# Retention and gated feed-forward on one core: weight pieces split over two DMA queues, queries loaded ahead of keys, and a new order of the first four chunks

## The chip, the cores and the metric

The kernel runs on one core of a Trainium2 chip. The metric is the device time of one execution in microseconds (us). The core's engines are TensorE (PE; PEld is its weight load), VectorE (DVE), ScalarE (ACT), GpSimd (POOL) and SyncE (SP). Each runs its own instructions in order, and they wait for each other by semaphores. SyncE, ScalarE and GpSimd can issue DMA transfers, each into a queue of its own; all transfers run on the core's 16 DMA engines. PSUM is the memory that TensorE writes.

## What is computed

A recurrent retention over 4 batches, 8 heads, 768 steps and a head size of 64, all in float32, and then a feed-forward block on its output, whose weights `w_in` (512 x 2048) and `w_out` (2048 x 512) come as float64.

```python
for t in range(S):
    state = gamma[None, :, None, None] * state + np.einsum('bhd,bhe->bhde', k[:, :, t], v[:, :, t])
    y[:, :, t] = scale * np.einsum('bhd,bhde->bhe', q[:, :, t], state)
x = y.transpose(0, 2, 1, 3).reshape(B * S, H * D)
h = x @ w_in
sp = np.maximum(h, 0.0) + np.log1p(np.exp(-np.abs(h)))
g = h * erf(sp)
return g @ w_out
```

## The kernel before

The 768 steps of a batch are six chunks of 128 steps, so there are 24 chunks. A chunk's retention is a few blocks of matmuls: its keys and queries are transposed, scores are formed and masked, and outputs and a state update follow. Two chunks make a group of 256 rows, the unit of the feed-forward block.

The first four chunks (`JPC = 4`) and the first two groups are worked off in an order that is written out by hand (lines 649 to 691). Its letters are functions of a chunk number j:

- `Q_` and `V_` (line 376, VectorE) scale the queries and the values by a power of the decay, in place; each waits for the transfer that brings them.
- `T(j, 0)` transposes the keys and `T(j, 1)` the queries: four matmuls against the identity (line 390) and a copy by ScalarE out of PSUM (line 396).
- `S_` (line 402) forms the scores, `M` (line 413, VectorE) masks them in two operations.
- `O_` (`ret_out`) multiplies the queries by the state (line 434; not for chunk 0), the masked scores by the values (line 441) and the keys by the values (line 449); ScalarE copies the result to x (line 454). A function given as `between` runs behind the first of these.
- `A` (line 459 or 461, VectorE) adds the new part to the state.
- `keep_warm(n)` runs n matmuls whose result nobody reads.

`w_in` is loaded in eight pieces of 256 columns, 1 MB each, into tiles `raw`. A piece has a lower half (partitions 0 to 63, r = 0) and an upper half (partitions 64 to 127, r = 1), each loaded by a transfer of its own. All of it is issued by SyncE: piece 0 in eight transfers of 128 KB, pieces 1 to 3 in four of 256 KB each, and the later ones in two of 512 KB once a buffer is free. In SyncE's queue stand, in this order, the keys and queries of chunks 0 to 3 (keys first) with the values of chunks 0 to 2 behind those of the next chunk, then part 0 of piece 0, the values of chunk 3, part 1 of piece 0, and pieces 1 to 3 (lines 272 to 283).

`conversion(n)` turns a piece of float64 words into float32. It is a generator, and each `next(weight_steps)` runs it up to its next `yield`. For pieces 0 to 3 a part is half of the columns, called a and b here. A part takes a mask of the exponent bits (line 184, VectorE), a scaling of the exponent by ScalarE (line 187), three operations on number and sign (lines 191, 196, 198), and the product (line 210). `need("in", ft)` runs steps until column block ft of 128 columns is ready: block 0 is part a of piece 0, block 1 is part b. When a piece's second part is nearly done, SyncE is told to load the piece four further on, and behind pieces 0 and 1 chunks 4 and 5.

`hidden_of(ft, g)` (line 591) multiplies group g by column block ft: four matmuls of 256 columns in float32. `put_hidden` copies the result to SBUF (line 599, ScalarE) and stores it by GpSimd's queue (line 601) into `hid`. From `hidden_of(1, 0)` on, a loop over ft from 0 to 15 runs these for groups 0 and 1, with the retention of chunks 4 and 5 (lines 497 to 572) and the splits of weights in between. Behind the loop come the other groups (line 616) and the second half of the feed-forward block (line 801).

Of the kernel before, what the change touches and what calls it, by code (L numbers as in the profile page):

```python
# [21 lines left out]
P = 128  # L22
C = 128
JPC = 4
# [17 lines left out]
def kernel(  # L42
# [13 lines left out]
    nc = tc.nc  # L56
    B, H, S, D = q.shape
# [5 lines left out]
    n_k = d_model // P  # L63
    n_ft = d_ff // P
    NPC = n_ft // 2
    DH = d_model // 2
# [13 lines left out]
    def b4(name, shape, dtype=F32):  # L80
        return big.tile([P] + shape, dtype, name=name, tag="b4")
# [4 lines left out]
    def b8(name, shape, dtype=F32):  # L86
        return wide.tile([P] + shape, dtype, name=name, tag="b8")
# [5 lines left out]
    KN, QN, V, KB, QB, KT, QT, SC, AM, SU = {}, {}, {}, {}, {}, {}, {}, {}, {}, {}  # L93
    KNP, VP = {}, {}

    def of_chunk(x, j):

        b, c = divmod(j, NC)
        return x[b, :, c * C : (c + 1) * C, :].rearrange("h p d -> p h d")

    def load(j):

        kq = b4("kq", [2, H, D])
        KN[j], QN[j] = kq[:, 0], kq[:, 1]
        for to, src in ((KN[j], k), (QN[j], q)):
            nc.sync.dma_start(to, of_chunk(src, j))  # L106

    def load_values(j):
        if j % 2 == 0:
            VP[j] = b4("v", [2, H, D])  # L110
        V[j] = VP[j - j % 2][:, j % 2]
        nc.sync.dma_start(V[j], of_chunk(v, j))
# [30 lines left out]
    WF, RAW, POWER = {}, {}, {}  # L143
    done = set()

    def load_piece(n, *parts):

        if n not in RAW:
            RAW[n] = b8("raw", [2 * d_model], I64)
        rows = (slice(2), slice(2, 4)) if n == 0 else (slice(4),)  # L150
        for part, g, r in itertools.product(parts or (None,), rows, range(2)):
            f = slice(2 * P) if part is None else slice(part * P, (part + 1) * P)
            nc.sync.dma_start(
                RAW[n][r * D : (r + 1) * D].rearrange("p (g f) -> p g f", g=n_k)[:, g, f],
                w_in[r * DH : (r + 1) * DH, n * 2 * P : (n + 1) * 2 * P].rearrange(
                    "(g p) f -> p g f", p=D
                )[:, g, f],
            )

    def load_quarter(i):  # L160

# [10 lines left out]
    def conversion(n):  # L172
# [5 lines left out]
        for part in range(2) if n < 4 else (None,):  # L178
# [22 lines left out]
            if part != 0:  # L201
                del RAW[n]
                if n + 4 < NPC:
                    load_piece(n + 4)
                if n < 2:
                    load(JPC + n)
                    load_values(JPC + n)
# [13 lines left out]
    def weights():  # L221


        for n in range(2 * NPC):
            yield from conversion(n)

    weight_steps = weights()
# [5 lines left out]
    def need(*what):  # L233
        while what not in done:
            next(weight_steps)
# [34 lines left out]
    nc.scalar.dma_start(d_k, decay_k)  # L270
    nc.scalar.dma_start(d_s, decay_s[::D].rearrange("(o s) h -> o s h", o=1).to_broadcast([P, 2, HP]))
    load(0)

    nc.scalar.copy(idle_out, ident[:, :1])

    for j in range(1, JPC):
        load(j)
        load_values(j - 1)
    load_piece(0, 0)
    load_values(JPC - 1)  # L280
    load_piece(0, 1)
    for n in range(1, 4):
        load_piece(n, 0, 1)

    causal = const.tile([P, C], F32, name="causal")
    nc.gpsimd.memset(causal, 1.0)
# [16 lines left out]
    def query_scale(c):  # L303
        nc.vector.reciprocal(kq_s[:, c, 1], kq_s[:, c, 0])
        nc.vector.tensor_scalar(kq_s[:, c, 1], kq_s[:, c, 1], unscale, None, op0=ALU.mult)
# [14 lines left out]
    def other_scales():  # L320
        query_scale(slice(2, NC))
# [30 lines left out]
    def keep_warm(n):  # L352
        for _ in range(n):
            nc.tensor.matmul(idle, ident, ident, start=True, stop=True)
# [3 lines left out]
    def ret_psum(pool=None):  # L358

        pool = pool or next(psum_turn)  # L360
        return pool.tile([P, HP, C], F32, name="hp" if pool is ps_h else "r")
# [3 lines left out]
    def x_of(j):  # L365

        g, i = divmod(j, 2)
        if i == 0:
            XC[g] = b4("xT", [HP, GT])
        return XC[g][:, :, i * C : (i + 1) * C]  # L370
# [13 lines left out]
    def ret_transpose(j, part=None, names=None):  # L384
        for i, (x, store) in enumerate(((KN[j], KT), (QN[j], QT))):
            if part not in (None, i):
                continue
            p = ps_o.tile([P, HP, C], F32, name=names[i]) if names else ret_psum(ps_h if i else ps_r)
            for u in range(HP):
                nc.tensor.transpose(  # L390
                    p[:, u, :], x[:, 2 * u : 2 * u + 2, :].rearrange("p h d -> p (h d)"), ident
                )
            if i == 0:
                KQT = b4("kqT", [2, HP, C])
                KT[j], QT[j] = KQT[:, 0], KQT[:, 1]
            nc.scalar.copy(store[j], p)
# [20 lines left out]
    def ret_out(j, between=None, state_last=False):  # L417
        c = j % NC
        x = x_of(j)
        pp = [ps_o.tile([P, HP, C], F32, name=f"o{(2 * j + r + 1) % 4}") for r in range(2)]  # L420

        def place(h):
            return pp[h % 2][h // 4 * D : (h // 4 + 1) * D, h % 4 // 2, :]

        if state_last:
            between()


        if c:
            for u in PAIRS:  # L430
                for r in range(2):
                    h = 2 * u + r
                    own = slice(r * D, (r + 1) * D)
                    nc.tensor.matmul(
                        place(h), state[own, u, :], QT[j][own, u, :],
                        start=(h % 4 < 2), stop=False, skip_group_check=True,
                    )
        if between is not None and not state_last:
            between()
        for h in (0, 4, 1, 5, 2, 6, 3, 7):  # L440
            nc.tensor.matmul(
                place(h), V[j][:, h, :], AM[j][:, h % 2, h // 2, :],
                start=(not c and h % 4 < 2), stop=True, skip_group_check=True,
            )

        new = SU[j] = pp[0][:, 2:, :].rearrange("p a (b d) -> p (a b) d", d=D)
        for h in range(H):
            r = h % 2
            nc.tensor.matmul(
                new[r * D : (r + 1) * D, h // 2, :], KN[j][:, h, :], V[j][:, h, :],  # L450
                start=False, stop=True, skip_group_check=True,
            )
        for r in range(2):
            nc.scalar.copy(x[:, r::2], pp[r][:, :2, :])
# [130 lines left out]
    def hidden_of(ft, g):  # L585

        if ft not in HP_:
            HP_[ft] = ps_h.tile([P, 2, GT], F32, name="hp")
        w = WF[ft // 2].rearrange("p h a f -> p (h a) f")
        for kk in range(n_k):  # L590
            nc.tensor.matmul(  # L591
                HP_[ft][:, g],
                w[:, kk, ft % 2 * P : (ft % 2 + 1) * P], XC[g][:, kk],
                start=(kk == 0), stop=(kk == n_k - 1),
            )
# [10 lines left out]
    def unit(g, n):  # L606
# [36 lines left out]

    Q_, V_, T, S_, M, O_, A = (
        scale_q, scale_v, ret_transpose, ret_scores, ret_mask, ret_out, ret_add
    )


    T(0, 0)
    keep_warm(2)  # L650
    Q_(0)
    second_scales()
    T(0, 1)
    keep_warm(1)
    T(1, 0)
    S_(0)
    Q_(1)
    T(1, 1)
    keep_warm(2)
    other_scales()  # L660
    M(0)
    V_(0)
    S_(1)
    Q_(2)
    O_(0)
    T(2, 0)
    M(1)
    A(0)
    T(2, 1)
    V_(1)  # L670
    Q_(3)

    def next_scores():
        S_(2)
        M(2)

    O_(1, next_scores)
    T(3, 0)
    V_(2)
    A(1)  # L680
    T(3, 1)
    need("in", 0)
    O_(2)
    S_(3)
    V_(3)
    next(weight_steps)
    A(2)
    M(3)
    need("in", 1)
    ret_out(JPC - 1, lambda: hidden_of(0, 0), state_last=True)  # L690
    hidden_of(1, 0)


# [217 lines left out]
    for n in range(NG * NU):  # L911
        g, i = divmod(n, NU)
# [62 lines left out]
```

## Time and profile before

| | us |
|---|---|
| median of 3 runs | 629.0 (628.09 to 629.4) |
| the profiled execution, time | 630.29 |
| the profiled execution, span | 628.6 |
| TensorE busy | 617.5 (98%) |
| VectorE busy | 472.9 (75%) |
| ScalarE busy | 346.8 (55%) |
| GpSimd busy | 99.8 (16%) |

The granted TensorE clock is 0.999 over the span. The page also says that SyncE's queue (q1) moved 67.53 MB, GpSimd's (q0) 37.77 MB and ScalarE's (q10) 0.14 MB. In the timelines of the engines, the first stretch reads as follows. TensorE's first transposes start at 4.61 us. VectorE scales the queries of chunks 0 to 3 at 5.96, 8.34, 11.96 and 15.58. It scales the values of chunk 2 at 18.89, starts converting part a of piece 0 at 20.71 and part b at 24.61. TensorE starts `hidden_of(0, 0)` at 23.68 and `hidden_of(1, 0)` at 29.10. Times within a timeline are counted from the start of the span, and "idle before" an instruction is put down to what ended it.

### The profile page before, as it was taken

The page shows a single profiled execution, that of the slowest core. Times are in us where ns is not written, and L with a number is a line of the kernel's source. Part 1 is how long each engine was busy: PE and PEld are TensorE (multiplying, and loading weights), DVE is VectorE, ACT ScalarE, POOL GpSimd, SP SyncE. Part 2 cuts the span into 40 slices and gives each one's busy share as a digit, 9 for nine tenths or more (in the row PEclk, how much of TensorE's full clock was granted, in tenths as well). Part 3 has the DMA queues.
Part 4 walks back from the last instruction along what each step waited for, and adds up shares of the span by engine and source line. Part 5 has one row for each costly group of instructions (what it writes and reads, how often), then busy time and mean ns, then how long its engine had stood idle before and what let it go on. Part 6 is the DMA issues. An engine that isn't in the chain of part 4 may idle for free.

```text
span 628.6 us, 14668 instructions
## 1 busy us (share of the span) xinstructions
PE 617.5 (98%) x6080; PEld 555.9 (88%) x6080; DVE 472.9 (75%) x608; ACT 346.8 (55%) x430; POOL 99.8 (16%) x189
## 2 busy tenths in 40 slices
PE   8899999999999999999999999999999999999997
PEld 7688789999999999999999978888888888888886
DVE  4887899849598887878777997867676686768650
ACT  3333353322323333232349779898889889888920
POOL 1054442222322413222111110000000000000000
PEclk9999999999999999999999999999999999999999
DMA  9999888986859898787945751453334314432300
GB/s 190 209 217 213 227 211 192 244 224 150 242 142 262 207 237 227 214 219 190 271 165 167 261 170 70 136 168 101 115 119 168 129 43 162 139 94 103 101 33 34
DMA packets 165426, 106.37 MB, mean 169 GB/s; under 512 B 139632, under 2 KB 143984, under 8 KB 165360
## 3 DMA queue, kind: packets, MB, share of 16 engines
q1 hardware_dynamic: 152608, 67.53, 44.4%
q0 software_dynamic: 12192, 37.77, 17.7%
q8 instruction: 47, 0.77, 0.5%
q10 hardware_dynamic: 560, 0.14, 0.1%
q14 instruction: 19, 0.16, 0.1%
HBM read 69.75 MB, written 35.65 MB: 168 GB/s over the span
## 4 chain that ended last, share of the span: by engine, by line
PE 89%; DMA 6%; SPq 2%; DVE 1%; issue 1%; POOL 1%; ACT 0%; DVEq 0%; POOLq 0%
PE o L616 35%; PE o L801 21%; PE hp L801 10%; PE r L801 10%; PE hp L591 4%; DMA hid<-h 3%; DMA kq_b<-decay_k_dram 2%; SPq L106 1%; DMA v<-in_v_dram 1%; PE hp L497 1%; PE hp L616 1%; PE r L616 1%; PE r L542 1%; DMA raw<-in_moe_w_in_dram 1%; PE hp L504 1%; PE r L553 1%
## 5 line engine op out<-in xcount | busy, mean ns | idle before, releaser
L616 PE MATMUL o<-x_hi,w_hi 128*128 128x256 f32 x600 | 149.6, 287 | 0.0
L616 PE MATMUL o<-x_lo,w_lo 128*128 128x256 f32 x600 | 147.2, 283 | 0.6 <-issue 0.6
L616 PEld LDWEIGHTS o<-x_hi,w_hi 128*128 128x128 f32 x600 | 115.0, 192 | 2.1 <-issue 0.7
L263 ACT ACTIVATE h<-o 128x512 f32<-128x512 f32 x75 | 44.7, 596 | 127.9 <-PE o L616 127.1
L616 PEld LDWEIGHTS o<-x_lo,w_lo 128*128 128x128 f32 x600 | 115.1, 192 | 0.1
L756 DVE TENSOR_TENSOR e<-hid,e 128x1024 f32<-128x1024 f32 x48 | 56.6, 1222 | 58.2 <-ACT e L746 58.2
L616 PE MATMUL o<-x_dif,w_dif 128*128 128x256 f32 x600 | 84.1, 283 | 0.0
L639 POOL DMA_DIRECT2D hid<-h x80 | 44.6, 558 | 206.7 <-DVE h L264 204.3
L616 PEld LDWEIGHTS o<-x_dif,w_dif 128*128 128x128 f32 x600 | 77.4, 192 | 0.0
L801 PE MATMUL o<-w_dif,g_dif 128*128 128x512 f32 x192 | 73.7, 389 | 0.0
L264 DVE SCALAR_TENSOR_TENSOR h<-o,h 128x512 f32<-128x512 f32 x75 | 51.2, 683 | 25.5 <-ACT h L263 13.1
L801 PE MATMUL o<-w_lo,g_lo 128*128 128x512 f32 x168 | 65.4, 389 | 0.0
L801 PE MATMUL o<-w_hi,g_hi 128*128 128x512 f32 x168 | 65.4, 389 | 0.0
L257 DVE SCALAR_TENSOR_TENSOR g_dif<-g_hi,g_lo 128x1024 fp32r<-128x1024 f32 x48 | 58.8, 1225 | 3.2
L255 ACT ACTIVATE g_hi<-e 128x1024 fp32r<-128x1024 f32 x48 | 51.0, 1063 | 17.8 <-DVE e L756 15.1
L256 DVE TENSOR_TENSOR g_lo<-e,g_hi 128x1024 fp32r<-128x1024 f32 x48 | 58.6, 1222 | 0.2
L591 PE MATMUL hp<-xT,w 128*128 128x256 f32 x256 | 56.9, 381 | 1.6 <-DVE w L210 1.6
L591 PEld LDWEIGHTS hp<-xT,w 128*128 128x128 f32 x256 | 48.1, 190 | 8.3 <-issue 1.2
L746 ACT ACTIVATE e<-e 128x1024 f32<-128x1024 f32 x48 | 48.2, 1053 | 0.3
L742 ACT ACTIVATE e<-hid 128x1024 f32<-128x1024 f32 x48 | 48.2, 1052 | 0.3
L801 PEld LDWEIGHTS o<-w_dif,g_dif 128*128 128x128 f32 x192 | 36.0, 188 | 7.5
L801 PE MATMUL hp<-w_dif,g_dif 128*128 128x512 f32 x96 | 37.5, 390 | 0.6 <-DVE h L264 0.6
(166 smaller groups left out, 1069.9 us busy)
## 6 DMA issues: line engine op xcount, KB each, us to landing
hid<-hid SPq DMA_DIRECT2D x48, 512.0 KB, 4.8
hid<-h POOLq DMA_DIRECT2D x80, 256.0 KB, 3.6
raw<-in_moe_w_out_dram POOLq DMA_DIRECT2D x32, 256.0 KB, 5.1
v<-in_v_dram SPq DMA_DIRECT2D x24, 256.0 KB, 5.7
out_dram<-y SPq DMA_DIRECT2D x23, 256.0 KB, 2.1
kb<-in_k_dram SPq DMA_DIRECT2D x144, 32.0 KB, 3.2
qb<-in_q_dram SPq DMA_DIRECT2D x144, 32.0 KB, 3.0
kn<-in_k_dram SPq DMA_DIRECT2D x18, 256.0 KB, 6.7
```

The source lines that it names most:

```text
L255: nc.scalar.activation(hi, x, AF.Copy, scale=KEEP)
L256: nc.vector.tensor_tensor(lo, x, hi.bitcast(F32), op=ALU.subtract)
L257: nc.vector.scalar_tensor_tensor(dif, hi.bitcast(F32), Z, lo.bitcast(F32), op0=ALU.mult, op1=ALU.subtract)
L263: nc.scalar.activation(to, a, AF.Copy, scale=1 + 1 / Z)
L264: nc.vector.scalar_tensor_tensor(to, b, -1 / Z, to, op0=ALU.mult, op1=ALU.add)
L591: nc.tensor.matmul(HP_[ft][:, g], w[:, kk, ft % 2 * P : (ft % 2 + 1) * P], XC[g][:, kk], start=(kk == 0), stop=(kk == n_k - 1),)
L616: nc.tensor.matmul(to[:, u], W[n][i][:, kk * 2 * P + u * P : kk * 2 * P + (u + 1) * P], X[g][i][:, kk], start=(u == 0 and kk == 0 and i == ...
L639: nc.gpsimd.dma_start(HID[g][:, 2 * n : 2 * n + 2], h)
L742: nc.scalar.activation(E[n], HID_[n], AF.Softplus)
L746: nc.scalar.activation(E[n], E[n], AF.Erf)
L756: nc.vector.tensor_tensor(E[n], HID_.pop(n), E[n], op=ALU.mult)
L801: nc.tensor.matmul(Y[g][t][x // 2], G[n][x][:, f, t * P : (t + 1) * P], W_OUT[ft // 2][x][:, ft % 2 * d_model : (ft % 2 + 1) * d_model], s ...
```

## The change

The queries of a chunk are loaded ahead of its keys. Pieces 0 to 3 of `w_in` are loaded half by half, with the four 64-row groups of a half in one transfer: the lower halves by SyncE, the upper halves by ScalarE. Piece 0 has two transfers of 256 KB for each half (its two parts), pieces 1 to 3 one of 512 KB. SyncE's queue now holds the lower half of part 0 of piece 0 ahead of the values of chunk 2, and the lower half of part 1 ahead of those of chunk 3. ScalarE issues its five transfers among its other work, at the calls of `upper`. The order of the first four chunks is new: the queries are transposed ahead of the keys, scores come earlier, and the steps of the weight conversion are spread among them. The later pieces are loaded as before.

```diff
-        for to, src in ((KN[j], k), (QN[j], q)):
+        for to, src in ((QN[j], q), (KN[j], k)):
             nc.sync.dma_start(to, of_chunk(src, j))
...
-    def load_piece(n, *parts):
+    def load_rows(n, r, part=None, queue=None):
 
         if n not in RAW:
             RAW[n] = b8("raw", [2 * d_model], I64)
-        rows = (slice(2), slice(2, 4)) if n == 0 else (slice(4),)
-        for part, g, r in itertools.product(parts or (None,), rows, range(2)):
-            f = slice(2 * P) if part is None else slice(part * P, (part + 1) * P)
-            nc.sync.dma_start(
-                RAW[n][r * D : (r + 1) * D].rearrange("p (g f) -> p g f", g=n_k)[:, g, f],
-                w_in[r * DH : (r + 1) * DH, n * 2 * P : (n + 1) * 2 * P].rearrange(
-                    "(g p) f -> p g f", p=D
-                )[:, g, f],
-            )
+        f = slice(2 * P) if part is None else slice(part * P, (part + 1) * P)
+        (queue or nc.sync).dma_start(
+            RAW[n][r * D : (r + 1) * D].rearrange("p (g f) -> p g f", g=n_k)[:, :, f],
+            w_in[r * DH : (r + 1) * DH, n * 2 * P : (n + 1) * 2 * P].rearrange(
+                "(g p) f -> p g f", p=D
+            )[:, :, f],
+        )
+
+    def load_piece(n):
+        for r in range(2):
+            load_rows(n, r)
...
     for j in range(1, JPC):
         load(j)
-        load_values(j - 1)
-    load_piece(0, 0)
-    load_values(JPC - 1)
-    load_piece(0, 1)
+        if j < JPC - 1:
+            load_values(j - 1)
+    for i in range(2):
+        load_rows(0, 0, i)
+        load_values(JPC - 2 + i)
     for n in range(1, 4):
-        load_piece(n, 0, 1)
+        load_rows(n, 0)
+
+    def upper(n, part=None):
+        load_rows(n, 1, part, nc.scalar)
...
-            if i == 0:
+            if j not in KT:
                 KQT = b4("kqT", [2, HP, C])
...
-    T(0, 0)
-    keep_warm(2)
     Q_(0)
     second_scales()
     T(0, 1)
-    keep_warm(1)
+    T(0, 0)
+    keep_warm(2)
+    Q_(1)
+    other_scales()
+    S_(0)
+    T(1, 1)
     T(1, 0)
-    S_(0)
-    Q_(1)
-    T(1, 1)
     keep_warm(2)
-    other_scales()
     M(0)
-    V_(0)
     S_(1)
     Q_(2)
+    V_(0)
+    T(2, 1)
+    T(2, 0)
+    upper(0, 0)
     O_(0)
-    T(2, 0)
+    upper(0, 1)
     M(1)
+    V_(1)
+    S_(2)
+    Q_(3)
     A(0)
-    T(2, 1)
-    V_(1)
-    Q_(3)
-
-    def next_scores():
-        S_(2)
-        M(2)
-
-    O_(1, next_scores)
-    T(3, 0)
+    M(2)
+    T(3, 1)
+    next(weight_steps)
+    O_(1, lambda: T(3, 0))
+    upper(1)
+    next(weight_steps)
     V_(2)
     A(1)
-    T(3, 1)
     need("in", 0)
+    S_(3)
     O_(2)
-    S_(3)
+    upper(2)
+    next(weight_steps)
+    M(3)
+    A(2)
     V_(3)
     next(weight_steps)
-    A(2)
-    M(3)
+    ret_out(JPC - 1, lambda: hidden_of(0, 0), state_last=True)
+    upper(3)
     need("in", 1)
-    ret_out(JPC - 1, lambda: hidden_of(0, 0), state_last=True)
     hidden_of(1, 0)
```

## The prediction

> **What bounds the kernel now.** I read the page's busy shares first, then TensorE's waits, then the chain of waits up to 70 us, then timelines and windows of that stretch.
>
> ```profile
> PE 617.5 (98%) x6080; PEld 555.9 (88%) x6080; DVE 472.9 (75%) x608; ACT 346.8 (55%) x430; POOL 99.8 (16%) x189
> ```
>
> TensorE is busy for 617.5 of 628.6 us. Its waits over the whole span, as engine, line and releaser, then total us, times and longest:
>
> ```profile
> PE hp L591 <- DVE w L210: 1.6, 2, 1.1
> PE o L354 <- POOL ident masks.py:199: 1.5, 1, 1.5
> PE o L434 <- DVE state L459: 1.4, 1, 1.4
> PE o L542 <- DVE state L524: 1.1, 1, 1.1
> ```
>
> Three of the four lie in the stretch that the change rewrites. The last is the only wait over 1 us behind it. So what moves the end is the start of the first uninterrupted run of L591 matmuls, plus that later wait. The chain (start, length, what) shows what sets both:
>
> ```profile
> 11.62 7.25 DMA v<-in_v_dram
> 18.88 0.59 SPq L153
> 19.52 4.97 DMA raw<-in_moe_w_in_dram
> 24.61 0.43 DVE power L184
> 28.26 0.70 DVE w L210
> 29.10 3.71 PE hp L591 x16
> 33.72 8.86 DMA hid<-h
> 45.65 9.58 DMA kq_b<-decay_k_dram
> 56.28 8.28 DMA hid<-h
> 64.69 0.76 DVE am L513 x2
> ```
>
> The opening is bound by loads in one queue. The issue at 18.88 begins when the values issued at 11.62 have landed (11.62 + 7.25), and SyncE issued eight transfers from the one to the other: an issue waits for the landing of the transfer eight before it. Then weight piece 0, part b lands at 24.49, VectorE converts it, and TensorE starts `hidden_of(1, 0)` at 29.10. After that the chain runs through GpSimd's stores and loads, each 8 to 10 us from issue to landing behind SyncE's backlog, and ends in the wait of 1.12 us at 64.7. The windows (us, busy time of PE, PEld, DVE, ACT, POOL, granted clock, DMA share, GB/s) show that backlog:
>
> ```profile
> 28.00:30.00 2.00, 0.90 (x4) 0.85 (x5) 1.93 (x6) 0.99 (x3) 0.00 (x0) 1.00 1.12 215
> 30.00:32.00 2.00, 2.00 (x11) 1.74 (x11) 1.97 (x4) 0.38 (x1) 0.00 (x0) 1.00 1.14 219
> 64.00:70.00 6.00, 4.88 (x86) 4.15 (x85) 5.24 (x9) 2.73 (x6) 3.43 (x7) 1.00 1.10 335
> ```
>
> Weight halves alone fill all DMA engines at 215 to 219 GB/s; at the same share, with GpSimd's stores mixed in, they move 335.
>
> **The change part by part.** *Queries ahead of keys.* VectorE starts the query scalings of chunks 1, 2 and 3 at 8.34, 11.96 and 15.58, when they land as transfers 4, 7 and 10: transfer n is seen at 3.5 + 1.21n. A query moves one place forward, so 1.2 us earlier. In the new order q2 is seen at 10.8, k2 at 12.0, q3 at 14.4, k3 at 15.6, then the lower half of 0a at 16.8, v2 at 18.0, the lower half of 0b at 19.2, v3 at 20.4. The earlier scalings gain nothing at the end: TensorE waits for weights later anyway. With that cover gone they would be worth up to 1.2 us. The warm-up matmuls go from five to four, 0.2 us under the same cover.
>
> *SyncE* issues 5 weight transfers instead of 20, at a median of 614 ns; ahead of 0b's completion that is two instead of eight, and the wait at 18.88 has no counterpart. What comes behind them in SyncE's queue (piece 4, chunk 4) waits for conversions at about 28 and is not late.
>
> *ScalarE* gets the other five, at 0.45 us (its own two small issues at 0.81 and 1.27) to 1.16 us (SyncE's issue at 12.80); I take 0.6, so 3.0 us. Only those ahead of a waited-for operation cost anything. After T(2,0), the first stands at about 13.4: keys 12.0, four transposes 0.5, latency 0.3, copy 0.6. If it counts as eighth after k3, it waits until 15.6, and behind it in ScalarE's queue stand the copies of O(0), the second upper half and the copy of T(3,1); TensorE next needs these copies for S(3), which waits for 0a anyway. If fewer of SyncE's issues count ahead of it, it waits less, down to nothing. I take 15.6, issued by 16.2.
>
> *When 0a is whole.* From issue to landing k0, with nothing ahead of it, took 3.2 us (the shortest of its tile); 15.6 + 3.2 = 18.8, and sharing the engines with the lower half of 0b adds up to 0.9 (that half's 1.2, less overlap). So 0a is seen at 18.9 to 19.7, against 20.71 now; at 16.9 without the wait; later if the upper half stands behind what SyncE has queued. The row for that is the store 33.72 + 8.86: unloaded, the same stores land in 3.6 us (minimum of L601), so 5 us were queueing. I take 19.7, nearer to the unloaded row: at 16 us keys and values of 256 KB per 1.2 us stand in the queue, not 512 KB halves.
>
> [...]
>
> *From 0a to the steady run.* Two chains, equally long. ScalarE and TensorE: power 0.46, exponent 0.72, copy of T(3,0) 0.49; then S(3) 1.1, O(2) 0.6 + 0.95 + 0.55, `hidden_of(0, 0)` 1.75, O(3) 2.1: 8.7 us. VectorE: power 0.35, number and sum 1.05, V(2) 0.6, A(1) 0.33, sign and product 1.3, power 0.35, M(3) 1.2, A(2) 0.35 after O(2), V(3) 0.6, number and sum 1.05, sign and product 1.3, with some 0.2 of latency: 8.7. The exponent of 0b stands behind the third weight issue on ScalarE (+0.6) and is ready at 7.1, where VectorE wants it at 7.3: hidden, with 0.2 to spare. Now the same distance is 29.10 - 20.71 = 8.4. So `hidden_of(1, 0)` starts at 19.7 + 8.7 = 28.4, a gain of 0.7, and break-even is 0a at 20.4. Part 0b does not decide: its lower half comes by 19.2, its upper one, issued at 17.6, about 21, and VectorE asks at 23.3.
>
> *Piece 1.* Now its part a (512 KB) suffices for the conversion at 29.20; in the change all 1 MB must be there. The upper half is issued at about 22.3, when the copies of O(1) are done. Sharing with the lower halves it lands at 26 to 27; behind all three (1.5 MB at 215 GB/s from 20.4, then its own 2.4) at 30 to 31. TensorE needs the converted part 3 x 1.73 = 5.2 after 28.4, VectorE 2.8 for it: landing by 30.8 is free. I count nothing, and up to 0.5 as the bound.
>
> *The wait at 64.7.* It ends with a store that landed 8.28 us after issue. The other queue takes 2 MB out of SyncE's, so piece 4 and chunk 4 no longer queue behind upper halves: 2 MB at 215 GB/s are 9.8 us of backlog. If both queues' halves overlap, as stores and halves do from 64 to 70, the backlog shrinks and the wait goes: 0 to 1.12; I take 1.0. What is late next is VectorE, but it idles 1.78 for v4 at 48.2, 1.86 at 58.1 and 2.29 before 64.69.
>
> *Sum.* 0.7 + 1.0 = 1.7 off the profiled execution: span 628.6 to 626.9, time 630.29 to 628.6. That execution stands 1.3 above the median of 629.0, so the median becomes 627.3. A measurement of this kernel can tell about 0.2%, 1.3 us, from no change.
>
> **The rivals.**
>
> *A. Larger gain.* ScalarE's issues wait for nothing and are served at once. 0a's landing moves from 19.7 towards 16.9, but the chain then waits for v2, which VectorE takes behind 0a's first steps: about 19.7 with the extra halves in front of it. So `hidden_of(1, 0)` starts at about 27.0, a gain of 2.1, with the 1.1: 625.8. For it: ScalarE's queue holds no other transfer. Against: SyncE's own wait at 18.88.
>
> *B. The halves do not overlap.* All transfers go on at 215 to 220 GB/s in sum, then the backlog up to 64 us is what it is now and the wait stays, moved with the opening: 0.2 to 0.8 off, 628.4. For it: from 28 to 32 halves saturate at that rate although lower and upper ones alternate in SyncE's queue. Against: the 335 GB/s, whose stores run the other way, however.
>
> [...]
>
> *C. Slower: the upper half of 0a is served behind what SyncE has queued.* SyncE has issued everything up to piece 3 by about 17 us, ScalarE not before 16. Behind v3 and the first of the lower 512 KB halves, 0a is seen at about 20.4 + 2.4 + 1.2 = 24.0, `hidden_of(1, 0)` starts at 32.7, 3.6 late; less the 1.1 the time is 631.5. It decides from 0a at 20.4 + 1.1 + 1.3 = 22.8, where slower can be told. Stalled behind all three halves it would be 5 us worse. For it: the three landings of 8 to 10 us that GpSimd's queue had beside SyncE's backlog. Against: these stood behind 512 KB and 256 KB weight transfers.
>
> **How the numbers follow.** Forecast 0.42, with its own range 626.3 to 628.2; A 0.13, B 0.22, C 0.23. Faster: four fifths of the forecast (0.34) and A: 0.47. Same: the rest of the forecast and most of B: 0.28. Slower: C and a tail of B where piece 1 is late: 0.25. The range reaches from just below A's 625.8 to the nearer half of C: 625.5 to 631.0.
>
> **What would show it.** Right: q0 scaled near 4.7; 0a's first VectorE step between 18.9 and 20.2; S(3) 1.7 after it; the first uninterrupted run of L591 at 28.0 to 28.8; no wait of TensorE above 0.3 us near 64; windows from 20 to 35 above 250 GB/s. B shows as 215 to 220 GB/s there and the wait still at 64. C shows as 0a's step after 22.8, with ScalarE idle ahead of its copies for the last transposes. Wrong in another way: a wait at L591 near 33 for piece 1, or a granted clock below 1.00 after TensorE's idle time before S(3), some 2.5 us where the longest now is 1.41.

## The result and the profile after

| | before | changed |
|---|---|---|
| median of five runs, us | 629.0 (628.09 to 629.9) | 636.29 (635.09 to 638.34) |
| the profiled execution, time / span | 630.29 / 628.6 | 636.10 / 634.4 |
| 0a / 0b (parts a and b of piece 0) seen by VectorE | 20.71 / 24.61 | 23.75 / 28.59 |
| run of `hidden_of(1, 0)` starts | 29.10 | 34.17 |
| TensorE's waits between 60 and 75 us | 1.12 | 1.26 + 0.46 |

The ratio is 1.0121, 95% interval 1.0097 to 1.0144: slower by 7.3 us. In the profiled executions the span grew by 5.8 (the one of the kernel before lies 1.3 above its median). The later start of the run is 5.07 of it, the waits are 0.60, so nearly all lies ahead of 75 us.

The page of the changed kernel: the busy times are what they were, and TensorE's share fell.

```profile
PE 618.3 (97%) x6078; PEld 556.0 (88%) x6078; DVE 473.1 (75%) x608; ACT 347.0 (55%) x430; POOL 100.1 (16%) x189
```

TensorE's waits (engine, line, releaser, then total us, times, longest):

```profile
PE r L408 <- ACT kqT L402: 7.6, 3, 7.1
PE o L360 <- POOL ident masks.py:199: 1.5, 1, 1.5
PE hp L597 <- ACT h L605: 1.3, 1, 1.3
...
PE o L548 <- DVE state L530: 0.5, 1, 0.5
```

The short waits in the opening have become one of 7.1 us ahead of S(3). Its releaser is ScalarE's copy of T(3, 0), which stands behind the exponent of 0a, so it is a wait for 0a. The later wait has not gone: it is now two. The chain of waits (start, length, what) shows both places:

```profile
14.03 9.70 DMA raw<-in_moe_w_in_dram
23.75 0.44 DVE power L186
24.21 0.61 ACT power L189
24.83 0.57 ACT kqT L402
25.45 0.58 PE r L408
...
34.19 3.69 PE hp L597 x16
37.90 0.60 ACT h L605
...
38.79 7.76 DMA hid<-h
...
58.20 8.24 DMA hid<-h
66.55 0.59 ACT h L605
67.13 1.05 ACT power L189
68.21 1.25 DVE power L200
...
70.62 0.75 DVE am L519 x2
```

The first line is ScalarE's upper half of 0a: issued at 14.03, whole 9.70 us later. Before, the chain had in its place a 128 KB transfer of part b of piece 0, issued at 19.52, which took 4.97. The timelines of SyncE's and ScalarE's DMA issues around it (start, length):

```profile
14.00 0.61 SPq L112 DMA_DIRECT2D v<-in_v_dram  x1
14.65 19.93 SPq L151 DMA_DIRECT2D raw<-in_moe_w_in_dram  x5
14.03 0.69 ACTq L151 DMA_DIRECT2D raw<-in_moe_w_in_dram  x1
17.88 0.60 ACTq L151 DMA_DIRECT2D raw<-in_moe_w_in_dram  x1
```

The values of chunk 3 (v3), issued by SyncE at 14.00, landed at 23.10; the upper half of 0a, issued by ScalarE 30 ns later, at 23.72. Issued at one time by the two engines, the two took about equally long. The upper half of 0b, issued at 17.88, landed at 28.57: ahead of it SyncE had issued the lower halves of pieces 1 (14.65) and 2 (17.52), 512 KB each. What the DMA queues moved (packets, MB, share of the engines), from 14 to 18 and then from 23 to 24, has a row for SyncE's queue q1 and none for ScalarE's, q10:

```profile
q1 hardware_dynamic: 1727, 0.78, 120.6%
```

```profile
q1 hardware_dynamic: 109, 0.20, 109.2%
```

So ScalarE's queue moved no packet of the upper half of 0a for 3.3 us behind the end of its issue (14.72), and in the second window none of the upper half of 0b, whose issue ended at 18.48, while SyncE's earlier transfers went on.

Part 0b is a second bound, beside the chain above. VectorE's first step and its product:

```profile
28.59 0.43 DVE L186 TENSOR_SCALAR power<-raw 128x512 uint32<-128x512 uint32 x1 [1.09 <-DMA raw<-in_moe_w_in_dram]
...
33.33 0.69 DVE L212 SCALAR_TENSOR_TENSOR w<-w,power 128x512 f32<-128x512 f32 x1
```

Between the two VectorE waits only 0.39, for TensorE's work, and the product is ready at 34.02, 0.15 ahead of the run. With 0a on time, 0b alone would still hold the run to about 33.8, an estimate from these rows.

The windows (us, busy time of PE, PEld, DVE, ACT, POOL, granted clock, DMA share, GB/s) show what the clock did behind TensorE's idle time:

```profile
20.00:22.00 2.00, 0.00 (x0) 0.00 (x0) 0.00 (x0) 0.00 (x0) 0.00 (x0) 0.97 1.15 218
22.00:24.00 2.00, 0.00 (x0) 0.00 (x0) 0.25 (x1) 0.00 (x0) 0.00 (x0) 0.50 1.08 202
24.00:26.00 2.00, 0.55 (x4) 0.55 (x6) 1.97 (x5) 1.74 (x4) 0.00 (x0) 0.50 1.06 228
26.00:28.00 2.00, 2.00 (x28) 1.77 (x28) 1.46 (x3) 0.00 (x0) 0.00 (x0) 0.50 1.09 305
28.00:30.00 2.00, 2.00 (x44) 1.67 (x36) 1.41 (x3) 0.00 (x0) 0.00 (x0) 0.82 1.08 226
```

TensorE's clock is halved from about 21.9 to 28.7, over S(3) and the first part of O(2). Between 26 and 28, when the upper half of 0b and the lower half of piece 2 are both under way, the engines move 305 GB/s; else 202 to 228.

### The profile page after: what moved, and what is told of

Same layout as the page of the kernel before. It is cut to its first block, busy times and chain, and to the rows that moved or that the text cites. A ratio compares the mean times of both kernels' runs of the same rounds, so it can differ in the third digit from the quotient of the medians.

```text
span 634.4 us, 14651 instructions
## 1 busy us (share of the span) xinstructions
PE 618.3 (97%) x6078; PEld 556.0 (88%) x6078; DVE 473.1 (75%) x608; ACT 347.0 (55%) x430; POOL 100.1 (16%) x189
## 3 DMA queue, kind: packets, MB, share of 16 engines
q10 hardware_dynamic: 1920, 2.24, 1.7%
## 4 chain that ended last, share of the span: by engine, by line
PE 90%; DMA 6%; SPq 1%; issue 1%; DVE 1%; ACT 1%; POOL 0%; DVEq 0%; ACTq 0%
PE o L622 35%; PE o L810 21%; PE hp L810 10%; PE r L810 10%; PE hp L597 4%; DMA hid<-h 3%; DMA raw<-in_moe_w_in_dram 2%; DMA kq_b<-decay_k_dram 1%; PE hp L503 1%; PE hp L622 1%; PE r L622 1%; DMA kq<-in_q_dram 1%; SPq L106 1%; PE r L548 1%; PE hp L510 1%; PE r L559 1%
## 6 DMA issues: line engine op xcount, KB each, us to landing
raw<-in_moe_w_in_dram SPq DMA_DIRECT2D x11, 512.0 KB, 10.4
```

## The experiments

The theory after the result: both hardware queues work off one backlog in order of issue, so an upper half that ScalarE issues late stands behind all that SyncE has issued (T). Rivals: the halves do not overlap; the new chunk order costs the time; ScalarE's own wait for the landing of an earlier transfer costs it. Ratios are to runs of the kernel before on the same chip, whose medians were 628.2 to 629.4.

**One part of the change alone.** The first kernel has the new order and queries first, with all weights issued by SyncE as before:

```diff
-    for i in range(2):
-        load_rows(0, 0, i)
-        load_values(JPC - 2 + i)
-    for n in range(1, 4):
-        load_rows(n, 0)
+    load_piece(0, 0)
+    load_values(JPC - 1)
+    load_piece(0, 1)
+    for n in range(1, 4):
+        load_piece(n, 0, 1)
...
-    upper(0, 0)
```

> The new order of the first four chunks and the queries ahead of the keys, with all weight halves issued by SyncE as in the kernel before (20 transfers). Theory (the upper half of 0a comes late because transfers of both queues are served in the order of issue): 0a is seen at 20 to 21.5, TensorE idles less than 2.5 us ahead of S(3), its clock stays at 1.00, hidden_of(1, 0) starts at 28.7 to 30, and the time is 628 to 630.5. Rival (the new order itself is at fault: the conversion of 0a stands ahead of V(2), and the copy of T(3,0) behind the exponent): the idle time ahead of S(3) stays above 5 us and the time is 634 or more.

Measured: 633.19 (628.33 to 636.23), ratio 1.0039 (1.0011 to 1.0067), where T had 628 to 630.5. The runs fall into two groups: five of 628.3 to 629.5 with a mean granted clock of 1.000, seven of 632.8 to 636.2 with 0.991 to 0.997. 0a is seen at 20.18. In the profiled run TensorE is idle for 3.65 ahead of S(3), and the clock is 0.50 from 21.5 to 28.3. Behind a wait of 2.38 near 66, 16 matmuls of L591 take 5.23, where 16 of them at 60.05 take 3.72. The second has only the queries ahead of the keys:

```diff
-        for to, src in ((KN[j], k), (QN[j], q)):
+        for to, src in ((QN[j], q), (KN[j], k)):
```

> The kernel before with the queries of a chunk loaded ahead of its keys, and nothing else. Theory: TensorE waits for weights later anyway, so 0a is seen at 20.7 as before and the time is 629 within 0.8. Rival (the order of the loads matters by itself): more than 1.3 us off 629 either way.

Measured: 628.13 (627.03 to 631.77), ratio 0.9991 (0.9972 to 1.001): nothing that can be told. The third keeps the order and the keys first and only splits the weights, with `upper` behind T(2, 0), T(2, 1), O(1), O(2) and the last output:

```diff
     T(2, 0)
+    upper(0, 0)
...
     T(2, 1)
+    upper(0, 1)
```

> The kernel before with the four pieces loaded in halves, the lower ones by SyncE in the new place ahead of the values of chunks 2 and 3, the upper ones by ScalarE behind T(2,0), T(2,1), O(1), O(2) and O(3); keys first and the old order of the chunks. Theory (service in the order of issue): the upper half of 0a is issued at 15 to 16, behind values and lower halves that SyncE has issued, 0a is seen at 23 to 26, hidden_of(1, 0) starts at 32 to 35 and the time is 632 to 637. Rival (the new order is at fault): 0a's lateness costs little in the old order, and the time is below 631.

Measured: 637.17 (636.63 to 638.33), ratio 1.0127 (1.0101 to 1.0153), as much as the whole change. 0a is seen at 21.45, earlier than T's 23 to 26 and only 0.74 later than before the change. 0b is seen at 29.11, 4.50 later, and the run, at 33.60, is 4.50 later too: here 0b alone makes the loss. The split is the cost; of the order, the first kernel shows no cost beside the clock.

**When the upper halves are issued.** The changed kernel with both upper halves of piece 0 behind T(1, 0):

```diff
     T(1, 0)
+    upper(0, 0)
+    upper(0, 1)
```

> The changed kernel with both upper halves of piece 0 issued by ScalarE behind T(1,0) instead of behind T(2,0) and O(0). Theory (service in the order of issue): issued at 10 to 12, they stand ahead of v2, v3 and pieces 1 to 3, 0a is seen at 17.5 to 20 and 0b by 23, TensorE idles under 3 us ahead of S(3), hidden_of(1, 0) starts at 27.5 to 30 and the time is 627 to 631. [...]

Measured: 635.06 (633.79 to 636.4), ratio 1.0091 (1.0065 to 1.0118), above T's 631. SyncE's queue is unchanged, but now the second upper half is issued (14.13) ahead of the lower half of piece 1 (15.57), and it lands at 22.85, not 28.57. So it is its place in line that counts, which the earlier issue gave it, not its 64 partitions and not its queue. 0a and 0b are seen at 20.43 and 24.10, as early as before the change, yet the run starts at 31.00, 1.90 later: the clock is 0.50 from 23.4 to 26.8, behind a gap of 1.82 us. With a wait of 0.52 for piece 1 that is 2.4 of the 3.5 us by which this profiled execution, the fastest of four, is longer than that of the kernel before. The rest of this kernel's loss is not accounted for. The next moves SyncE's lower halves of pieces 1 to 3 to where the upper ones are called:

```diff
+    load_rows(1, 0)
     upper(1)
```

> The changed kernel, with SyncE's lower halves of pieces 1 to 3 no longer issued ahead but each right before the upper half of its piece (behind O(1), O(2) and the last chunk's output). Left as it is: the upper half of 0a, which in the changed kernel was issued at 14.02 and landed at 23.72. Theory of order of issue: the lower halves of pieces 1 to 3 (14.65, 17.52, 18.18) were issued behind upper(0,0), so 0a comes no more than 0.5 us earlier (23.2 to 23.7), while upper(0,1), issued at 17.88, has only v3 and nothing of pieces 1 and 2 ahead of it and lands near 25 in place of 28.57; piece 1 then comes some 9 us after its issue near 24, at 32 to 33, as it does now; time 634 to 636.3. [...]

Measured: 636.14 (634.41 to 637.89), ratio 1.0124 (1.0098 to 1.015). The edit did not do what I meant: SyncE does not wait for ScalarE, so its issues for pieces 1 and 2 came at 15.87 and 17.47, still ahead of upper(0, 1) at 17.91, which landed at 28.67. But v3's issue ended at 15.83, behind that of upper(0, 0) (14.85), and 0a came 1.9 us earlier, at 21.84. I had expected at most 0.5 of T. Order by the end of the issue agrees: one 256 KB transfer less stands ahead, which is 1.2 us at the spacing of the keys and queries; the other 0.7 is not accounted for. And the time is that of the changed kernel, for 0b is as late as there and TensorE waits for its product:

```profile
33.79 22.68 PE L595 MATMUL hp<-xT,w 128*128 128x256 f32 x104 [0.93 <-DVE w L212]
```

To take SyncE's backlog away for certain, ScalarE issues the lower halves too:

```diff
+    load_rows(1, 0, None, nc.scalar)
     upper(1)
```

> The changed kernel, with the lower halves of pieces 1 to 3 issued by ScalarE right before their upper halves; SyncE then has nothing after v3 and cannot run ahead. Upper(0,0) is issued at about 14, upper(0,1) at about 17.9, as before the edit. Theory of order of issue: ahead of upper(0,0) stand the lower half of 0b and v3, so it lands at 21.5 to 23.5; ahead of upper(0,1) stands nothing that is not already there, so it lands at 23.5 to 25.5 in place of 28.57, 5 to 7 us after its issue in place of 10.7, and VectorE sees 0b then. Piece 1, issued at some 22 to 24 with nothing ahead, lands by 31. Time 630.5 to 634.5. [...]

Measured: 631.05 (627.54 to 637.11), ratio 1.0032 (1.0012 to 1.0052). The profiled execution is the longest of the ten, so only its transfers are read here. The upper half of 0b lands at 23.44, as T said. Part of that is an earlier issue: 14.19 and not 17.88, right behind ScalarE's copy at 14.18 and with no wait for a landing. Last, the changed kernel with the second queue gone and nothing else:

```diff
         load_rows(0, 0, i)
+        load_rows(0, 1, i)
         load_values(JPC - 2 + i)
     for n in range(1, 4):
-        load_rows(n, 0)
+        load_piece(n)
```

> The changed kernel, with the upper halves issued by SyncE right behind the lower ones; sizes, chunk order and queries first as in the changed kernel, only the second queue and its late places go. Theory of order of issue: 0a's upper half is issued some 0.7 us behind its lower half and nothing else is ahead of it, so VectorE has 0a at 19.5 to 20.5 and 0b at 23.5 to 24.5, as with the new chunk order alone (20.18); TensorE's idle time ahead of S(3) is 3 to 4 us again, and the time is that of the new order alone, 628.3 to 629.5 where the clock holds and 632.8 to 636 where it falls, median 629 to 634. [...] Theory that the new chunk order is what costs the time: 635 to 637, whatever 0a does.

Measured: 629.16 (627.44 to 632.09), ratio 1.0008 (0.9991 to 1.0025). With the same sizes, order and queries the loss is gone: it came from issuing the upper halves by ScalarE, which is late with them. The transfers of the upper halves side by side, as issue and landing:

| kernel | 0a | 0b | large halves issued ahead of 0b's |
|---|---|---|---|
| changed | 14.03, 23.72 | 17.88, 28.57 | 14.65 and 17.52 |
| split alone | 14.17, 21.42 | 17.44, 29.09 | 15.43 and 16.98 |
| lower halves called late | 14.16, 21.82 | 17.91, 28.67 | 15.87 and 17.47 |
| upper halves early | 12.92, 20.41 | 14.13, 22.85 | none |
| lower halves on ScalarE | 12.69, 21.48 | 14.19, 23.44 | none |
| all on SyncE | 12.87, 19.06 | 16.04, 23.12 | none |

ScalarE's own wait is a part of the cause and not a rival to it. In the changed kernel its copies ahead of the second issue were done at 15.41, but the issue began at 17.88, when the lower half of 0a had landed (17.86). By then SyncE had issued the lower half of piece 1 and was issuing that of piece 2. No run takes this wait away and leaves all else as it is.

**The clock.** Matmuls of the identity fill TensorE's idle time ahead of S(3), which overwrites their output:

```diff
+        for _ in range(50 if j == 3 else 0):
+            nc.tensor.matmul(pp[0][:, 0, :], ident, ident, start=True, stop=True)
```

> The changed kernel, with 50 more matmuls of the identity on TensorE (about 0.11 us each at the full clock, 5.5 us in all) ahead of S(3), where TensorE is idle for 7.07 us; their output is overwritten by S(3). No transfer changes. Theory that the idle time itself costs the clock (granted 0.50 from 22 to 28 us): the clock stays at 0.95 or more up to 30 us, S(3) takes 1.1 us in place of 2.0, the run of hidden_of(1,0) starts at 32.5 to 33 in place of 34.17, and the time falls by 1.3 to 2 us, to 634.3 to 635. Theory that the granted clock follows something else than the idle time (the load of the memory, the start of the heavy run): clock and time stay as in the changed kernel, 636.3 within 0.7.

Measured: 639.0 (638.3 to 639.03), ratio 1.0167 (1.0145 to 1.0189). The clock held (0.999), but a matmul took 0.227 us, not 0.11, and S(3) had to wait until 30.00. From there to the run took 7.26 us at the full clock and with 0b there (30.26), against 8.72 in the changed kernel (25.45 to 34.17). The same on the new order alone, with 25, overran too:

> The new chunk order with the queries first and the weights all from SyncE as in the kernel before (its runs lay in two groups: five at 628.3 to 629.5 with a mean granted clock of 1.000, seven at 632.8 to 636.2 with 0.991 to 0.997), and 25 more matmuls of the identity ahead of S(3), 2.7 us of the 3.65 us in which TensorE is idle there; S(3) overwrites their output. Theory that this gap costs the clock: all runs have a clock of 0.999 or 1.000 and lie at 628.0 to 629.7, level with the kernel before (ratio 0.997 to 1.001). Theory that the clock falls for another reason: two groups again, median 631 to 634.

Measured: 634.55 (633.82 to 635.72), ratio 1.0102 (1.0083 to 1.0121), S(3) at 24.16, the run at 31.42, again 7.26 later. In two of its six runs the clock was 0.996 all the same, which the theory does not have. With 24 in the changed kernel:

> The changed kernel with 24 more matmuls of the identity on TensorE ahead of S(3), in place of the 50 of the run before: those took 0.227 us each and kept TensorE till 30.07, 4.6 us past the moment at which S(3) could start. 24 are 5.4 us, from 18.7 to 24.1, inside the 7.07 us in which TensorE is idle in the changed kernel; their output is overwritten by S(3). Theory that the idle time costs the clock and the clock costs time: granted clock 0.95 or more from 22 to 30, S(3) at 25.0 to 25.5, the run of hidden_of(1,0) 7.2 us later (as with 50, from 30.07 to 37.28), at 32.2 to 33.0 in place of 34.17, and 634.2 to 635.2 us. Theory that the clock costs nothing that shows, since the weights' own lateness (0b at 28.6) sets the run: run at 33.8 or later, time within 0.7 of 636.3.

Measured: 637.79 (637.56 to 638.08), ratio 1.015 (1.0132 to 1.0168): a miss, and a useful one. In this execution v3's issue ended at 15.74, behind that of the upper half of 0a (14.77), though no transfer was edited, and 0a was seen at 21.60 already. The filling kept TensorE about 1 us past the copy of T(3, 0), which ended at 23.26. TensorE's timeline:

```profile
24.30 0.37 PE L410 MATMUL r<-kqT 64*128 64x128 f32 x1
...
27.47 1.99 PE L599 MATMUL hp<-xT,w 128*128 128x256 f32 x8
31.70 1.13 PE L442 MATMUL o<-kqT,state 64*64 64x128 f32 x16 [2.24 <-DVE state L467]
...
35.31 0.92 PE L599 MATMUL hp<-xT,w 128*128 128x256 f32 x3
```

S(3) starts at 24.30, 1.15 earlier than in the changed kernel, and all goes well up to `hidden_of(0, 0)`. Then TensorE waits 2.24 for a state update that stands in VectorE's order behind the first step of 0b, and 0b is not there before 29.70. The clock falls there instead (0.50 from 32 to 34), and the run starts at 35.31, 1.14 later than in the changed kernel. So 0b's lateness is a bound of its own, right behind 0a's, as the second theory had it, though the time is 0.8 above that theory's range. The new order alone with 12 such matmuls, which end ahead of 0a:

> The new chunk order with the queries first and the weights all from SyncE as before (two groups: 628.3 to 629.5 with a mean granted clock of 1.000, and 632.8 to 636.2), and 12 more matmuls of the identity ahead of S(3), 2.7 us at 0.227 us each, inside the 3.65 us of its idle time there (25 took 5.8 us and held S(3) from 20.9 to 24.2). Theory that the idle time costs the clock and the clock the slower group: clock 0.999 or 1.000 in all runs, all at 628 to 629.8. Theory that the groups come from elsewhere: runs above 632 remain, with a clock below 0.998.

Measured: 629.32 (628.19 to 632.29), ratio 1.0004 (0.9985 to 1.0023), a clock of 0.999 or 1.000 in all twelve runs, one of them above 632. Windows of the new order alone, then of this kernel:

```profile
22.00:24.00 2.00, 2.00 (x20) 1.78 (x24) 1.97 (x5) 0.38 (x2) 0.00 (x0) 0.50 1.01 242
```

```profile
22.00:24.00 2.00, 2.00 (x40) 1.71 (x42) 1.97 (x5) 0.33 (x2) 0.00 (x0) 1.00 1.12 245
```

TensorE is busy throughout in both and does twice as many matmuls in the second. S(3) starts at 21.89 and 21.83, the run at 31.99 and 29.09: the clock is worth 2.8 us there. The medians are 3.9 apart, but from two chips, and the intervals of the two ratios overlap. The group of runs with a low clock is gone; four of the twelve still lie above the 629.8 of the theory. On the kernel with the lower halves on ScalarE, with 16:

> The changed kernel with the lower halves of pieces 1 to 3 on ScalarE (three runs at 627.5 to 628.3 with a clock of 0.999 or 1.000, six at 630.9 to 632.9 with 0.993 to 0.997), and 16 more matmuls of the identity ahead of S(3), 3.6 us at 0.227 us each of the 4.59 us idle there. Theory that the clock makes the groups: all runs at 627.0 to 628.8, level with the kernel before or 0.1 to 0.2% faster (0a at 21.5, 0b at 25.2 against 24.6, S(3) at 23.2). Theory that the groups come from elsewhere: median 630 or more.

Measured: 630.15 (628.76 to 632.88), ratio 1.002 (1.0003 to 1.0037). The clock held but for one run (0.997), and the runs are closer together, yet none is below 628.7. The ratio is 0.0012 lower than without the filling, which the two intervals do not tell from nothing, and not the gain that I expected. Why it is not level with the kernel before is not settled.

**The wait near 65 us.** GpSimd issues 17 loads of block scales from 35 to 52, and the stores of h queue behind them. They read inputs, so they can go to 8 us, here on the kernel before:

```diff
     other_scales()
+    load_block_scales()
...
-        1: [(load_block_scales,)],
```

> The kernel before, with GpSimd's 17 loads of the block scales (by_b and the 16 of kq_b, from inputs) issued at some 8 us, where GpSimd is idle, in place of 35 to 52, where the stores of h queue behind them. Theory that this queue sets the wait in the middle (ScalarE's third h waits for the landing of the stores of the first, VectorE's masks and states behind it): TensorE's wait of 1.12 us near 64.7 goes and time falls by 0.8 to 1.2 us, to 627.5 to 628.3, if the early loads cost nothing; if they slow the first keys and queries (some 2,000 packets of 4 bytes beside them), the start of the run of hidden_of(1,0) moves from 29.10 to 30 or later and the time rises by as much. Theory that the stores wait for the memory and not for their queue: the wait near 64.7 stays at 1 us or more, time unchanged, 629 within 0.7.

Measured: 630.29 (629.41 to 631.24), ratio 1.003 (1.002 to 1.0041). The wait is gone: TensorE waits for nothing between 31 and 75. But 0b is now seen at 26.26, not at 24.61, and the run starts at 30.75, 1.65 later. Behind the product of 0a, on the kernel with queries first:

```diff
     need("in", 0)
+    gate = const.tile([P, 1], F32, name="gate")
+    nc.gpsimd.tensor_copy(gate, WF[0][:, 0, 0, :1])
+    load_block_scales()
```

> The kernel before with the queries ahead of the keys (628.13, 627.03 to 631.77), and GpSimd's 17 loads of the block scales issued from some 24.5 us, when 0a's product is done (GpSimd copies one column of it first), in place of 34.5 to 51. Moved to 8 us they took the wait near 64 away and cost 1.65 us at the start of the run of hidden_of(1,0). Theory that the wait in the middle is GpSimd's queue alone: no wait of TensorE over 0.3 us between 35 and 75, run of hidden_of(1,0) at 28.4 to 28.9, time 626.3 to 627.5. Theory that the loads cost as much wherever they meet weights: run at 29.5 or later, or a wait of 0.5 us or more for piece 1 or 2 between 30 and 45, time 628 to 629.5.

Measured: 627.94 (627.42 to 628.88), ratio 0.9981 (0.9957 to 1.0004): the lowest median of all, and not shown to be faster. The run starts at 28.30, as the first theory had it. The waits of this kernel:

```profile
PE hp L591 <- DVE w L210: 1.5, 2, 0.9
PE o L354 <- POOL ident masks.py:199: 1.5, 1, 1.5
PE r L390 <- DMA kq<-in_k_dram: 0.9, 1, 0.9
```

The row of L542 is gone, but a new wait of 0.93 for VectorE's product stands at 57.3; the chain of waits runs there through a transfer of later values that landed at 51.6. On the changed order with one queue and 9 filling matmuls the same gave no gain:

> The changed kernel with both halves on SyncE (629.16, 627.44 to 632.09; run of hidden_of(1,0) at 29.70, TensorE's wait near 65 of 0.69 us), with the block scales' loads behind 0a's product as in the run before, and 9 more matmuls of the identity (2.0 us) in the 2.34 us of idle time ahead of S(3). If clock and GpSimd's queue are what is left: clock 0.999 or 1.000, no wait between 35 and 75, 627.0 to 628.5. If the loads of the scales cost weights: piece 1 (seen at 30.47 there) comes later than 31.2 and the time stays at 629 or more.

Measured: 629.68 (628.44 to 632.92), ratio 1.0012 (0.9991 to 1.0033). And the loads in halves by SyncE in the old order:

> The kernel before, with the queries ahead of the keys and piece 0 to 3 loaded by SyncE in the halves of the changed kernel (lower, upper, then the values of chunks 2 and 3 behind 0a and 0b); the chunk order stays as it was. With the changed kernel's chunk order these loads gave 0a at 19.15, 0b at 23.14, a run of hidden_of(1,0) at 29.70 and 629.16 (627.44 to 632.09). Theory that the chunk order costs and the loads help: 0a at 19.2, the run at 27.6 to 28.5 in place of 29.10, time 627.0 to 628.5. Theory that after the start the order in GpSimd's queue decides (kq_b loads, then the stores of the first h, then ScalarE's third h): whatever the start gains is lost in the wait near 64, time within 1 us of the kernel before, 628.0 to 630.

Measured: 632.65 (630.81 to 638.03), ratio 1.007 (1.0041 to 1.01): a miss of both theories. 0a landed at 17.90, but VectorE took it at 21.85, because in the old order it first scales v2, which now stands behind 0a and landed at 20.89. Six of its seven runs had a clock of 0.993 to 0.997. The new loads need the new order.

## Why the prediction was wrong

I forecast 627.3, and the range ended at 631.0. In kind the result is rival C, and larger than its 631.5.

- **Two terms failed. The first is "when 0a is whole": 15.6 + 3.2.** The issue came earlier than I thought, at 14.03: it waited for q3 (landed 14.00) and not for k3 (15.4). But the transfer took 9.7 us, not 3.2 plus at most 0.9. I had chosen the row of k0, which had nothing ahead of it. My own chain showed the row that fits: v2, issued at 11.62, took 7.25 us. SyncE's queue was not empty when ScalarE issued: the lower halves of 0a and 0b landed at 17.86 and 20.7, v2 at 19.4 and v3 at 23.10. 0a was seen at 23.75, where C had 24.0 and the point from which it decides was 22.8.
- **The second is "Part 0b does not decide".** Its upper half landed at 28.57, not about 21, behind two lower halves of 512 KB that I had let stand in SyncE's queue without counting them ahead of it. This one alone makes most of the loss. In the kernel with the split alone 0a is 0.74 late and the run 4.50; with the lower halves called late 0a comes 1.9 earlier than in the changed kernel, and the run 0.38. With 24 filling matmuls 0b costs 2.24 us of TensorE's time at once. The chain from 0a reaches the run just as late, at 34.17; no run puts 0b right and leaves 0a as late as it was.
- **"Sharing the engines", "adds up to 0.9".** The two queues did not share them from the issue on: 23.72 beside SyncE's 23.10 for an issue at the same moment, and not one packet of ScalarE's queue from 14 to 18 us, while SyncE's moved 1727. Why ScalarE's queue stood still the trace does not show. The one-queue kernel, at 629.16 against 636.29, shows no gain from the second queue.
- **"From 0a to the steady run", 8.7 us, took 10.4.** The two chains were worked out at the full clock. I named the clock among the things that would make the prediction wrong, with an idle time of 2.5; it was 7.07. S(3) comes 3.62 later than with the new order and the clock kept (25.45 against 21.83; there the run begins at 29.09, as before the change), and from S(3) to the run takes 8.72 instead of 7.26. The 1.46 is not the clock's alone: at the full clock 0b would have held the run to about 33.8 against 34.17, so the clock by itself is worth some 0.4 here.
- **The wait at 64.7, "I take 1.0", did not go.** I put it down to SyncE's backlog. With the scales moved the wait is gone in two kernels, so it hangs on GpSimd's own order: the stores of h stand behind loads that wait for landings (in the kernel before, eight transfers are issued from 33.72 on, and the ninth, at 42.86, begins when the first has landed, at 42.58). In the changed kernel all of this is shifted by 5 us, ScalarE waits 7.65 for a store ahead of its copy of h, and the exponent, VectorE's product and the masks stand behind that.
- **Rival B is out as the cause.** Halves in both queues moved 305 GB/s together (26 to 28 us), against 202 to 228 otherwise: 34% over the 228, in the window of 2 us in which both are being moved, and four other kernels with two queues have 293 to 314 there. Nor do the 215 to 219 GB/s that spoke for B show a limit of halves: from 10 to 12 us, when only keys, queries and values are loaded, over all 128 partitions, the changed kernel moves 217 too.
- **Right:** q2 was scaled at 10.50 and q3 at 14.03 (10.8 and 14.4 forecast), an issue by ScalarE took 0.60 to 0.69 (0.6), the queries' place was worth nothing that the times can tell, and piece 1 cost no wait here (0.52 in the kernel with the upper halves early).

## What to carry to other kernels

Here, moving half of a load to another engine's queue did not move it out of line. So compare the moment of its issue with all that every other queue has issued by then, and take the price from a transfer issued at the same moment (v3: 9.1 us), not from an unloaded one (k0: 3.2 us). ScalarE, with work of its own between its issues, lost its place to SyncE, which issued ahead (14.65 and 17.52 against 17.88). And where one part comes late, ask whether the next one would hold the same operation: 0b did, behind 0a. A wait of TensorE is to be counted with the clock behind it: with the upper halves early, 1.82 us of idle time were followed by 3.4 us at 0.50.

## What was not expected of the hardware

- The two queues behaved nearly as one line, ordered by the end of the issue: v3 issued until 14.61 (SyncE) and the upper half of 0a until 14.72 (ScalarE) landed at 23.10 and 23.72; with 15.83 and 14.85 they landed at 23.75 and 21.82. The order is not strict: with 50 filling matmuls the ends were 14.63 and 14.70 and the landings 24.23 and 23.94.
- The clock's low stretches (0.50) lasted about 3.4 us or twice that: 21.5 to 24.9 with all on SyncE, 23.4 to 26.8 with the upper halves early, 21.9 to 28.7 in the changed kernel, 21.5 to 28.3 with the new order alone. An idle time of 1.82 us (upper halves early), 2.24 (24 filling matmuls) or 2.34 (all on SyncE) was followed by one, while 2.31 (25 filling matmuls, near 64) was not: the 16 matmuls behind it took 3.72. With the same program it came in some runs and not in others: three of 35 runs of the kernel before, on one chip, have a mean clock of 0.995 to 0.997.
